# Three token tiles, not two, share the first pass over the up weights

## The chip, the cores and the metric

The kernel runs on one core of a Trainium2 chip. The metric is the device time of one execution in microseconds (us). Engines named below: PE (TensorE, matmuls), DVE (VectorE), ACT (ScalarE), POOL (GpSimd) and SP (SyncE, which issues most transfers).

## The reference

For x of 2048 tokens by 512 features (bf16) the kernel gives x + A(xn) + B(xn), where xn is the layer norm of x over the features without gain or bias:

```
A: Bu = xn @ B_bar^T              complex, 512 states
   h_t = Lam_bar * h_(t-1) + Bu_t over the 2048 tokens
   y   = 2 Re(h @ C^T) + xn * Dskip
B: (silu(xn @ w_gate) * (xn @ w_up)) @ w_down      inner width 1376
```

## The kernel before

Tokens are cut into four chunks of 512, a chunk into four tiles of 128. For chunks 1 to 3 everything is done feature by feature on a transposed chunk. The first tiles of chunk 0 are done token by token, because their work can start before all weights have arrived: a tile of x, transposed on PE against the identity matrix and freed of its mean, is the stationary operand, and a row block of weights, 128 of the 512 input features by 512 columns, is the moving one (`sw_mm`, L503, one matmul for each k, group and tile). The scale of the layer norm (rstd) is applied afterwards, when ACT empties PSUM: `sw_up` (L522) for up, `sw_gate` (L512) for gate. The weight columns stand in three groups: groups 0 and 1 of 512 columns each (`wu01`, `wg01`, loaded row by row, `load_row`, L121), and group 2 of 352 (`w_end`).

In the front, tiles 0 and 1 go together. `raw_mm` (L240) transposes them on PE, `cT_mean` (L244) subtracts the mean by a second matmul into the same PSUM bank, and `raw_copy` (L248), shared by ACT and DVE, brings the centered tile to SBUF. `row_mm` (L747) then does one weight row for both tiles and both groups, four matmuls; the four up rows come first, then the four gate rows. Tile 2 is centered by DVE (`center`, L225), transposed on PE between gate rows 2 and 3, and does its groups 0 and 1 in the list of tile visits (L813), which goes on to group 2 of tiles 0 to 2 and to all of tile 3. The prologue also makes the layer norm's statistics (`ln_stats`, `ln_rstd`), normed tiles (`norm_dve`) and their DMA transposes (`xT0_dma`, L257) for chunk 0, transposes the small parameters on PE (`prm_transpose`, `prm_copy`), and starts the transposed loads of B's two halves (`load_bt`, L148). PE needs B's first half when the visits are done and the projections of chunk 0 (`bproj_tile`, L382) begin.

The order on each engine is the order in which the program is written; there is no scheduler behind it. DVE's and ACT's longer work (tables of sines, statistics and norms of later chunks, the scan `ssm_ops`, the 8 steps `c_ops` that build CF from C) stands in one list, `backlog`. `pump(us)` (L677) is called after every piece of PE work with that piece's length, and takes items from the list as long as the sum of pumped time covers their written costs; `need(tag)` (L691) forces what must be there. An item may have a first part (`pre`), placed up to two items earlier; for CF it is ACT's scaling `cm` (L370), on which DVE's step (L373) waits. A visit of the list at L813 pumps

```
pump(2 * KD * (fgroups[gi][1] - fgroups[gi][0]) * 128 / CW * 0.2163)
```

The norms of a chunk are followed by its DMA transpose (`xT_dma`, L261), for which the projection of that chunk waits. Chunk 3's bias (`ln_nb`, L202), its four norms on ACT (`norm_act`, L212) and its transpose come from the list while PE does the output of chunk 0 (`out_ffn`, `out_ssm`; ACT copies the results, L652); the projection of chunk 3 follows.

Of the kernel before, what the change touches and what calls it, by code (L numbers as in the profile page):

```python
# [11 lines left out]
BF16 = mybir.dt.bfloat16  # L12
ALU = mybir.AluOpType
# [10 lines left out]
def kernel(  # L24
# [17 lines left out]
    nc = tc.nc  # L42
    _, L, D = A_x.shape
# [6 lines left out]
    NCH = L // CW  # L50
    TPC = CW // 128
    KD = D // 128
# [15 lines left out]
    const = ctx.enter_context(tc.tile_pool(name="const", bufs=1))  # L68
# [9 lines left out]
    def bank(shape=(128, CW), dtype=F32):  # L78
        return psum.tile(list(shape), dtype, name="ps")
# [4 lines left out]
    x_v = A_x[0].rearrange("(n p) d -> p n d", p=128)  # L84
# [5 lines left out]
    xall = const.tile([128, NT, D], BF16, name="xall")  # L90
    xnT = const.tile([128, NCH, KD, CW], BF16, name="xnT")
# [29 lines left out]
    def load_row(q, t, view, k):  # L121
        q.dma_start(out=t[:, k, :], in_=view[:, k, 0:FE])  # L122

    HK = KD // 2
    ident = const.tile([128, 128], BF16, name="ident")
    make_identity(nc, ident[:])
    minus_mean = const.tile([128, 128], BF16, name="minus_mean")
# [3 lines left out]
    nc.scalar.preload_act_table_set("silu_and_others")  # L131
    for k in range(KD):
        load_row(nc.sync, wu01, wu_v, k)
    for k in range(HK):
        load_row(nc.sync, wg01, wg_v, k)
    nc.sync.dma_start(out=xall[:, 2, :], in_=x_v[:, 2, :])
    load_row(nc.sync, wg01, wg_v, HK)
    nc.sync.dma_start(out=xall[:, 3, :], in_=x_v[:, 3, :])
    load_row(nc.sync, wg01, wg_v, HK + 1)
# [34 lines left out]
    mv = const.tile([128, NT, 2], F32, name="mv")  # L174
# [10 lines left out]
    def by_k(ap):  # L185
        return ap.rearrange("p (k d) -> p k d", d=128)

    def ln_stats(n):
        nc.vector.bn_stats(out=stats[:, n, 0, :], in_=xall[:, n, :])  # L189
        nc.vector.bn_aggr(out=mv[:, n, :], in_=stats[:, n, 0, :])  # L190
# [6 lines left out]
    def ln_rstd(a, b):  # L197
        nc.vector.tensor_scalar(out=ve[:, a:b], in0=mv[:, a:b, 1], scalar1=EPS, scalar2=None, op0=ALU.add)  # L198
        nc.gpsimd.tensor_tensor(out=rstd[:, a:b], in0=ve[:, a:b], in1=neg_half[:, 0:b - a], op=ALU.pow)  # L199
# [5 lines left out]
    def norm_dve(n):  # L205
        c, i = divmod(n, TPC)
        nc.vector.tensor_scalar(out=xn_tile(c)[:, :, i, :], in0=by_k(xall[:, n, :]), scalar1=mv[:, n, 0:1],
                                scalar2=rstd[:, n:n + 1], op0=ALU.subtract, op1=ALU.mult)
# [9 lines left out]
    SW = TPC - 1  # L218
# [1 line left out]
        return flat(ap).rearrange("p (i k d) -> p k i d", k=KD, i=TPC)  # L220

    xn_c[0], xnT0 = rows_first(xc), rows_first(xnT[:, 0])
    sums = const.tile([128, 2], BF16, name="sums")

    def center(i):  # L225
        nc.vector.tensor_scalar(out=xc[:, i, :], in0=xall[:, i, :], scalar1=mv[:, i, 0:1], scalar2=None, op0=ALU.subtract)

    def sum_dve(i, dst):
        nc.vector.scalar_tensor_tensor(out=xnT[:, NCH - 1, i, 0:HW], in0=xall[:, i, 0:HW], scalar=1.0,
                                       in1=xall[:, i, HW:D], op0=ALU.mult, op1=ALU.add, accum_out=dst)  # L230

    pair = [[[bank() for _ in range(2)] for _ in range(2)] for _ in range(2)]
    warm = pair[0][0][1]
    raw = [pair[0][1] + pair[1][0], pair[1][1] * 2]

    def cT_mm(ps, src, k, first, stop):
        nc.tensor.matmul(ps[:, k * 128:(k + 1) * 128], lhsT=src[:, k * 128:(k + 1) * 128], rhs=ident[:], start=first,  # L237
                         stop=stop)

    def raw_mm(i):  # L240
        for k in range(KD):
            cT_mm(raw[i][k], xall[:, i, :], k, all(p is not raw[i][k] for p in raw[i][:k]), False)

    def cT_mean(i, *ks):  # L244
        nc.tensor.matmul(by_k(raw[i][ks[0]][:])[:, ks[0]:ks[-1] + 1:HK], lhsT=sums[:, i:i + 1].to_broadcast([128, 128]),
                         rhs=minus_mean[:, None, :].to_broadcast([128, len(ks), 128]), start=False, stop=True)

    def raw_copy(i, k):  # L248
        cT_copy(V.tensor_copy if k % 2 else nc.scalar.copy, raw[i][k], i, k, k + 1)

    def cT_copy(copy, ps, i, k0=0, k1=KD):
        copy(out=xcT[:, k0:k1, i * 128:(i + 1) * 128], in_=by_k(ps[:, k0 * 128:k1 * 128]))

    def runs(ap):
        return ap.rearrange("p k (i t) -> p (k i) t", t=128)
# [1 line left out]
    def xT0_dma(i0, i1):  # L257
        nc.sync.dma_start_transpose(out=flat(xnT[:, 0])[:, i0 * D:i1 * D].rearrange("p (n t) -> p n t", t=128),
                                    in_=flat(xc)[:, i0 * D:i1 * D])
# [14 lines left out]
    V = nc.vector  # L274

    def prm_transpose():
        pp = bank()[:, 0:128]
        nc.tensor.matmul(pp, lhsT=prm_rows[:], rhs=ident[:], start=True, stop=True)  # L278
        return pp

    def prm_copy(pp):
        V.tensor_copy(out=prm[:].rearrange("p t q -> p (t q)"), in_=pp[:, 0:3 * NQ])

    def exp_pool(out, in_):
        nc.gpsimd.tensor_tensor(out=out, in0=e_t[:], in1=in_, op=ALU.pow)

    def params_a():
        V.tensor_tensor(out=dre[:], in0=dt_t[:], in1=lre, op=ALU.mult)
        exp_pool(r_t[:], dre[:])
        V.scalar_tensor_tensor(out=ws2[:, 0, :], in0=dt_t[:], scalar=INV_2PI, in1=lim, op0=ALU.mult, op1=ALU.mult)  # L290
# [212 lines left out]
    def sw_mm(ps, groups, gi, i, k0=0, k1=KD):  # L503
        a, b = fgroups[gi]
        for k in range(k0, k1):
            nc.tensor.matmul(ps[:, 0:(b - a) * 128], lhsT=tokens(i, k), rhs=groups[gi][:, k, 0:(b - a) * 128],  # L506
                             start=(k == 0), stop=(k == KD - 1))
# [14 lines left out]
    def sw_up(gi, i, psu):  # L522
        key, h, w = u_home(gi, i)
        if key not in u_pair:
            u_pair[key] = up_p.tile([128, 2, CW], BF16, name="u2")
        nc.scalar.activation(out=u_pair[key][:, h, 0:w], in_=psu[:, 0:w], func=ACT.Copy, scale=sw_scale(i))

    def sw_out(gi, i, psg, psu):
        a, b = fgroups[gi]
        key, h, w = u_home(gi, i)  # L530
        sw_gate(gi, i, psg)
        if psu is not None:
            sw_up(gi, i, psu)
        if h == 1:
            if key[-3:] == "g01":
                g = g0[:, 0:b, i, :].rearrange("p (h f) d -> p h f d", h=2)
                u = u_pair[key][:].rearrange("p h (f d) -> p h f d", d=128)
            else:
                g = g0[:, a:b, i - 1:i + 1, :]
                u = u_pair[key][:, :, 0:w].rearrange("p i (f d) -> p f i d", d=128)  # L540
            products.append(lambda: V.tensor_tensor(out=g, in0=g, in1=u, op=ALU.mult))
# [185 lines left out]
    dummy(warm, 4, CW)  # L727
    dummy(warm, 5, 128)
    nc.vector.tensor_scalar(out=minus_mean[:], in0=ident[:], scalar1=-1.0 / D, scalar2=None, op0=ALU.mult)
    for i in range(2):  # L730
        sum_dve(i, sums[:, i:i + 1])
    raw_mm(0)
    for k in range(HK):
        cT_mean(0, k)
        raw_copy(0, k)
    raw_mm(1)
    for k in range(HK, KD):
        cT_mean(0, k)
    for k in range(HK):
        cT_mean(1, k, k + HK)  # L740
        raw_copy(1, k)
    for k in range(HK, KD):
        raw_copy(0, k)
    for k in range(HK, KD):
        raw_copy(1, k)

    def row_mm(which, k):  # L747
        for i in range(2):
            for gi in range(2):
                sw_mm(pair[which][i][gi], (U, G)[which], gi, i, k, k + 1)  # L750

    for k in range(KD):
        row_mm(0, k)
    for i in range(2):
        ln_stats(i)
        ln_rstd(i, i + 1)
    for gi in range(2):
        for i in range(2):
            sw_up(gi, i, pair[0][i][gi])
    for n in range(2):  # L760
        norm_dve(n)
    row_mm(1, 0)
    pp = prm_transpose()
    ln_stats(2)
    center(2)
    ln_rstd(2, 3)
    ln_stats(3)
    ln_rstd(3, 4)
    prm_copy(pp)
    exp_pool(dt_t[:], ldt)  # L770
    for k in range(1, SW):
        row_mm(1, k)
    t2 = bank()
    for k in range(KD):
        cT_mm(t2, xc[:, 2, :], k, k == 0, k == KD - 1)
    cT_copy(nc.scalar.copy, t2, 2)
    row_mm(1, SW)
    for i in range(2):
        sw_out(0, i, pair[1][i][0], None)
    norm_dve(SW)  # L780
    xT0_dma(SW, TPC)
    norm_dve(2)
    xT0_dma(0, SW)
    params_a()
    load_bt(0)
    load_bt(1)
    nc.gpsimd.iota(out=jidx[:], pattern=[[1, CW]], base=0, channel_multiplier=0,
                   allow_small_or_imprecise_dtypes=True)
    for i in range(2):
        sw_out(1, i, pair[1][i][1], None)  # L790
    tables = table_ops()
    stats1, norm1 = ln_rest(1, False)
    queue("tables", tables[:1])
# [16 lines left out]
        sw_mm(psu, U, gi, i)  # L810
        return psg, psu

    for gi, i in [(0, 2), (1, 2), (2, 0), (2, 1), (2, 2), (0, 3), (1, 3), (2, 3)]:  # L813
        sw_out(gi, i, *sw_both(gi, i))
        if (gi, i) == (2, 0):
            params_sin()
        pump(2 * KD * (fgroups[gi][1] - fgroups[gi][0]) * 128 / CW * 0.2163)
        multiply(1)
# [126 lines left out]
```

## Time and profile before

| | us |
|---|---|
| median of 3 runs | 177.92 (177.83 to 178.49) |
| profiled execution | 178.12 |
| its span, first to last instruction | 176.0 |

The numbers of the trace below come from the profiled execution, counted from the start of its span; its time lies 0.2 above the median and 2.1 above its span. In a row of the timeline stand the start, the length, the engine (PEld: loading of stationary operands; SPq: a transfer issued by SP), the line, the operation, what is written and read, the shape, the number of merged instructions, and in brackets the idle time before and what ended it. A row of the waits has the sum, the count and the longest; a row of the groups has the busy time, the mean in ns, and the idle time before; a row of the transfers ends with the time from issue to landing.

### The profile page before, as it was taken

The numbers are of one execution on the slowest core, as the hardware profiler recorded it, in microseconds if no ns is written. First come the engines' busy times: TensorE is split into PE (matmuls) and PEld (weight loads), VectorE is DVE, ScalarE is ACT, GpSimd is POOL, SyncE is SP. The second block draws the span as 40 slices with busy tenths as digits, with TensorE's granted clock in tenths as the row PEclk, the third lists the DMA queues.
The fourth block names the chain that finished last, engine by engine and source line by source line (L and its number), as shares of the span: only waits on it lengthen the run. The fifth ranks groups of instructions, "written<-read, shape, count | busy, mean of one in ns | idle before, by whom it ended". The sixth has DMA issues, their size and how long they took to land.

```text
span 176.0 us, 2435 instructions
## 1 busy us (share of the span) xinstructions
PE 171.0 (97%) x878; PEld 82.0 (47%) x894; DVE 157.4 (89%) x260; ACT 102.3 (58%) x188; POOL 27.1 (15%) x36
## 2 busy tenths in 40 slices
PE   8899999999999999999999999999999999999993
PEld 5444445564444464444444444446444444444542
DVE  3767999999999999999999999999999999589642
ACT  3179589794996689976044362014666652983100
POOL 5234110022000000000302500014100000530700
PEclk9999999999999999999999999999999999999999
DMA  5998969999999300220005830006310000597741
GB/s 152 370 342 80 194 110 181 303 202 293 169 207 274 115 4 0 50 61 0 2 4 111 94 34 0 0 4 68 53 22 0 0 4 0 70 164 124 93 89 60
DMA packets 34027, 18.05 MB, mean 103 GB/s; under 512 B 24512, under 2 KB 32832, under 8 KB 33888
## 3 DMA queue, kind: packets, MB, share of 16 engines
q1 hardware_dynamic: 30272, 14.39, 35.0%
q0 software_dynamic: 3456, 3.28, 14.6%
q10 hardware_dynamic: 288, 0.23, 0.4%
q8 instruction: 7, 0.11, 0.3%
q14 instruction: 4, 0.03, 0.1%
HBM read 8.33 MB, written 5.24 MB: 77 GB/s over the span
## 4 chain that ended last, share of the span: by engine, by line
PE 94%; DMA 3%; issue 1%; SPq 0%; ACT 0%; DVE 0%; ACTq 0%
PE ps L462 29%; PE ps L630 20%; PE ps L643 16%; PE ps L387 16%; PE ps L506 7%; PE ps L555 3%; DMA wu<-in_B_w_up_dram 3%; PE ps L805 2%; PE ps L620 2%; ACT u L489 0%; SPq L122 0%; SPq L128 0%; DVE xall L646 0%; PE ps L237 0%; PE ps L278 0%
## 5 line engine op out<-in xcount | busy, mean ns | idle before, releaser
L429 DVE TENSOR_TENSOR_SCAN g<-r_t,car,u 128x512 bf16<-128x512 f32 x24 | 28.8, 1263 | 0.0
L643 PE MATMUL ps<-CF,wt 128*128 128x512 bf16 (+2 forms) x133 | 28.2, 366 | 0.2
L387 PE MATMUL ps<-xnT,BT 128*128 128x512 bf16 x125 | 28.1, 379 | 0.2
L630 PE MATMUL ps<-wd_sb,guT 128*128 128x512 bf16 (+2 forms) x129 | 26.5, 362 | 0.1
L462 PE MATMUL ps<-xnT,wu 128*128 128x512 bf16 x94 | 24.5, 379 | 0.2
L462 PE MATMUL ps<-xnT,wg 128*128 128x512 bf16 x93 | 24.3, 379 | 0.1
L389 ACT CAST u<-ps 128x512 bf16<-128x512 f32 x32 | 17.8, 591 | 5.0 <-PE ps L387 4.1
L489 ACT CAST u<-ps 128x512 bf16<-128x512 f32 x30 | 17.8, 592 | 4.8 <-PE ps L462 4.8
L643 PEld LDWEIGHTS <-wt 128*128 128x128 bf16 x136 | 12.9, 98 | 15.0 <-DVE xall L600 0.4
L387 PEld LDWEIGHTS <-BT 128*128 128x128 bf16 x128 | 12.5, 98 | 14.9 <-DMA BT<-in_A_B_re_dram 0.3
L630 PEld LDWEIGHTS <-guT 128*128 128x128 bf16 x130 | 12.4, 98 | 13.8
L199 POOL TENSOR_TENSOR rstd<-ve,neg_half 128x1 f32<-128x1 f32 (+1 forms) x7 | 7.0, 1001 | 73.0 <-DVE ve L198 72.6
L652 ACT CAST res<-ps 128x512 bf16<-128x512 f32 x12 | 6.9, 582 | 18.5 <-PE ps L643 18.5
L592 ACT ACTIVATE xr<-xall,nb,rstd 128x512 bf16<-128x512 bf16 x16 | 11.8, 804 | 8.7 <-DVE xall L600 5.0
L653 POOL DMA_DIRECT2D out_dram<-res x12 | 10.5, 1043 | 35.6 <-ACT res L652 30.0
L462 PEld LDWEIGHTS <-wu 128*128 128x128 bf16 x96 | 9.4, 98 | 11.3
L488 ACT ACTIVATE guT<-ps 128x512 bf16<-128x512 f32 x20 | 12.1, 604 | 4.0 <-PE ps L462 3.6
L462 PEld LDWEIGHTS <-wg 128*128 128x128 bf16 x96 | 9.3, 98 | 10.6
L212 ACT ACTIVATE xn<-xall,nb,rstd 128x512 bf16<-128x512 bf16 x8 | 6.3, 816 | 8.8 <-DVE nb L202 8.8
L189 DVE BATCH_NORM_STATS2 stats<-xall 128x6 f32<-128x512 bf16 x16 | 10.8, 675 | 0.6 <-DMA xall<-in_A_x_dram 0.6
L462 PE MATMUL ps<-xnT,w_end 128*128 128x512 bf16 x47 | 10.8, 379 | 0.1
L397 DVE TENSOR_TENSOR pm<-g,c 128x2048 bf16<-128x2048 bf16 x8 | 9.8, 1222 | 0.1
(132 smaller groups left out, 235.3 us busy)
## 6 DMA issues: line engine op xcount, KB each, us to landing
out_dram<-in_A_x_dram SPq DMA_DIRECT2D x8, 192.0 KB, 3.2
out_dram<-res POOLq DMA_DIRECT2D x12, 128.0 KB, 3.1
out_dram<-xall POOLq DMA_DIRECT2D x3, 512.0 KB, 6.4
wd_sb<-in_B_w_down_dram SPq DMA_DIRECT2D x1, 1280.0 KB, 7.8
wu<-in_B_w_up_dram SPq DMA_DIRECT2D x4, 256.0 KB, 4.9
wg<-in_B_w_gate_dram SPq DMA_DIRECT2D x4, 256.0 KB, 5.5
xall<-in_A_x_dram SPq DMA_DIRECT2D x1, 1024.0 KB, 7.0
xall<-in_A_x_dram SPq DMA_DIRECT2D x1, 512.0 KB, 6.1
```

The costliest lines, as they stand in the source:

```text
L189: nc.vector.bn_stats(out=stats[:, n, 0, :], in_=xall[:, n, :])
L387: nc.tensor.matmul(ps[:] if c else by_k(ps[:]), lhsT=BT[:, part, k, q * 128:(q + 1) * 128], rhs=xnT[:, c, k, :] if c else xnT0[:, k], star ...
L389: nc.scalar.copy(out=u_tiles[c][:, part, q, :], in_=ps[:])
L429: V.tensor_tensor_scan(out=g()[:, part, q, :], data0=r_t[:, q:q + 1].to_broadcast([128, CW]), data1=u_tiles[c][:, part, q, :], initial=ini ...
L462: nc.tensor.matmul(ps[:fs, lo:hi], lhsT=wslice(groups, fi, k), rhs=xnT[:, c, k, lo:hi], start=(k == 0), stop=(k == KD - 1))
L488: nc.scalar.activation(out=gu(c, fi, fi + 1)[:fs, 0, :], in_=psg[:fs], func=ACT.Silu)
L489: nc.scalar.copy(out=u_pair[c][:fs, fi % 2, :], in_=psu[:fs])
L506: nc.tensor.matmul(ps[:, 0:(b - a) * 128], lhsT=tokens(i, k), rhs=groups[gi][:, k, 0:(b - a) * 128], start=(k == 0), stop=(k == KD - 1))
L592: nc.scalar.activation(out=box["xr"][:], in_=xall[:, n, :], func=ACT.Identity, scale=rstd[:, n:n + 1], bias=nb[:, n:n + 1])
L630: nc.tensor.matmul(o_tiles[n, b][:, 0:hi - lo], lhsT=gu(c, fi, fi + 1)[:, 0, i * 128:(i + 1) * 128], rhs=wd_sb[:, fi, lo:hi], start=(fi == ...
L643: nc.tensor.matmul(o[:, 0:hi - lo], lhsT=w_tiles[c][:, part, q, i * 128:(i + 1) * 128], rhs=CF[:, part, q, lo:hi], start=False, stop=(part ...
L653: nc.gpsimd.dma_start(out=out_v[:, n, lo:hi], in_=res[:, lo:hi], accum_op=ALU.add)
```

## The change

- Tile 2 of x is loaded on SP's queue between up rows 0 and 1, before it came after gate row 1.
- Tiles 0, 1 and 2 share the passes over up and gate. Six PSUM banks hold up, and gate tiles reuse banks. For row 0, tiles 0 and 1 go first; tile 2's transposes, copies, mean and row 0 follow; rows 1 to 3 go over three tiles.
- The mean is no longer added in PSUM by matmuls into the transposed tile. `raw_copy` now copies the raw transposed tile on ACT alone, in two halves; one matmul for each tile (`mean_mm`) makes the negative mean, and DVE adds it (`centered`). `center` and tile 2's later transposes are gone.
- Gate runs tile by tile instead of row by row, each tile over all four rows.
- The parameters' transpose stands behind up row 2, their copy behind tile 0's statistics; all statistics of chunk 0 come before its norms.
- The visits (0, 2) and (1, 2) leave the list of tile visits, and with them their calls of `pump`.

```diff
+        if k == 0:
+            nc.sync.dma_start(out=xall[:, 2, :], in_=x_v[:, 2, :])
     for k in range(HK):
         load_row(nc.sync, wg01, wg_v, k)
-    nc.sync.dma_start(out=xall[:, 2, :], in_=x_v[:, 2, :])
...
+    upb0 = [bank() for _ in range(2)]
+    raw = [bank() for _ in range(SW)]
+    low01, low2 = bank(), bank()
+    upb = [upb0, raw[0:2], [raw[2], bank()]]
+    gateb = [[low01, low2], upb[0], upb[1]]
+    xrT = xnT[:, NCH - 2]
...
+    def raw_copy(i, h):
+        k0, k1 = h * HK, (h + 1) * HK
+        nc.scalar.copy(out=xrT[:, k0:k1, i * 128:(i + 1) * 128], in_=by_k(raw[i][:, k0 * 128:k1 * 128]))
+    def mean_mm(i):
+        nc.tensor.matmul(mean_of(i), lhsT=sums[:, i:i + 1].to_broadcast([128, 128]), rhs=minus_mean[:], start=i != 1,
+                         stop=i != 0)
+    def centered(i, k0, k1):
+        at = slice(i * 128, (i + 1) * 128)
+        V.tensor_tensor(out=xcT[:, k0:k1, at], in0=xrT[:, k0:k1, at],
+                        in1=mean_of(i)[:, None, :].to_broadcast([128, k1 - k0, 128]), op=ALU.add)
...
+    for i in range(2):
+        raw_mm(i)
+        mean_mm(i)
+        for h in range(2):
+            raw_copy(i, h)
     for k in range(HK):
+        for i in range(2):
+            centered(i, k, k + 1)
+    for i in range(2):
+        for gi in range(2):
+            up_mm(i, gi, 0)
+    raw_mm(2)
+    for h in range(2):
+        raw_copy(2, h)
+    sum_dve(2, sums[:, 2:3])
+    mean_mm(2)
     for k in range(HK):
+        centered(2, k, k + 1)
+    for gi in range(2):
+        up_mm(2, gi, 0)
+    for i in range(SW):
+        centered(i, HK, KD)
+    for k in range(1, KD):
+        for i in range(SW):
             for gi in range(2):
+                up_mm(i, gi, k)
+        if k == HK:
+            pp = prm_transpose()
+    for i in range(SW):
         ln_stats(i)
         ln_rstd(i, i + 1)
+        if i == 0:
+            prm_copy(pp)
+            exp_pool(dt_t[:], ldt)
+    for i in range(SW):
+        for k in range(KD):
+            for gi in range(2):
+                sw_mm(gateb[i][gi], G, gi, i, k, k + 1)
+        if i < 2:
+            for gi in range(2):
+                sw_up(gi, i, upb[i][gi])
     ln_stats(3)
     ln_rstd(3, 4)
+    for n in (0, 1, SW, 2):
+        norm_dve(n)
+        if n == SW:
+            xT0_dma(SW, TPC)
     xT0_dma(0, SW)
+    for gi in range(2):
+        sw_out(gi, 0, gateb[0][gi], None)
+    for gi in range(2):
+        sw_up(gi, SW - 1, upb[SW - 1][gi])
+    for gi in range(2):
+        sw_out(gi, 1, gateb[1][gi], None)
...
-    for gi, i in [(0, 2), (1, 2), (2, 0), (2, 1), (2, 2), (0, 3), (1, 3), (2, 3)]:
+    for gi, i in [(2, 0), (2, 1), (2, 2), (0, 3), (1, 3), (2, 3)]:
```

More of the change, by code (lines that the diff above doesn't have):

```diff
@@ L222 @@
     xn_c[0], xnT0 = rows_first(xc), rows_first(xnT[:, 0])
-    sums = const.tile([128, 2], BF16, name="sums")
-    def center(i):
-        nc.vector.tensor_scalar(out=xc[:, i, :], in0=xall[:, i, :], scalar1=mv[:, i, 0:1], scalar2=None, op0=ALU.subtract)
+    sums = const.tile([128, SW], BF16, name="sums")
     def sum_dve(i, dst):
@@ L230, in sum_dve @@
                                        in1=xall[:, i, HW:D], op0=ALU.mult, op1=ALU.add, accum_out=dst)
-    pair = [[[bank() for _ in range(2)] for _ in range(2)] for _ in range(2)]
-    warm = pair[0][0][1]
-    raw = [pair[0][1] + pair[1][0], pair[1][1] * 2]
+    upb0 = [bank() for _ in range(2)]
[3 more added lines that the diff above has]
+    gateb = [[low01, low2], upb[0], upb[1]]
+    warm = upb0[0]
+    xrT = xnT[:, NCH - 2]
     def cT_mm(ps, src, k, first, stop):
@@ L241, in raw_mm, with mean_of @@
         for k in range(KD):
[L242 to L252, printed above, removed]
+            cT_mm(raw[i], xall[:, i, :], k, k == 0, k == KD - 1)
+    def raw_copy(i, h):
+        k0, k1 = h * HK, (h + 1) * HK
+        nc.scalar.copy(out=xrT[:, k0:k1, i * 128:(i + 1) * 128], in_=by_k(raw[i][:, k0 * 128:k1 * 128]))
+    def mean_of(i):
+        return low2[:, 0:128] if i == SW - 1 else low01[:, i * 128:(i + 1) * 128]
+    def mean_mm(i):
[5 more added lines that the diff above has]
+                        in1=mean_of(i)[:, None, :].to_broadcast([128, k1 - k0, 128]), op=ALU.add)
     def runs(ap):
@@ L276, in prm_transpose @@
     def prm_transpose():
-        pp = bank()[:, 0:128]
+        pp = low2[:, 128:256]
         nc.tensor.matmul(pp, lhsT=prm_rows[:], rhs=ident[:], start=True, stop=True)
@@ L729, with up_mm @@
     nc.vector.tensor_scalar(out=minus_mean[:], in0=ident[:], scalar1=-1.0 / D, scalar2=None, op0=ALU.mult)
+    def up_mm(i, gi, k):
+        sw_mm(upb[i][gi], U, gi, i, k, k + 1)
     for i in range(2):
         sum_dve(i, sums[:, i:i + 1])
-    raw_mm(0)
-    for k in range(HK):
[L734 to L738, printed above, removed]
-    for k in range(HK):
[L740 to L748, printed above, removed]
+    for i in range(2):
[3 more added lines that the diff above has]
+            raw_copy(i, h)
+    for k in range(HK):
+        for i in range(2):
[8 more added lines that the diff above has]
+    mean_mm(2)
@@ L749, in row_mm @@
+    for k in range(HK):
+        centered(2, k, k + 1)
[5 more added lines that the diff above has]
+        for i in range(SW):
             for gi in range(2):
[L750 to L754, printed above, removed]
+                up_mm(i, gi, k)
+        if k == HK:
+            pp = prm_transpose()
+    for i in range(SW):
@@ L755 @@
         ln_stats(i)
         ln_rstd(i, i + 1)
[L757 to L766, printed above, removed]
+        if i == 0:
[8 more added lines that the diff above has]
+                sw_up(gi, i, upb[i][gi])
@@ L767 @@
     ln_stats(3)
     ln_rstd(3, 4)
[L769 to L782, printed above, removed]
-    xT0_dma(0, SW)
+    for n in (0, 1, SW, 2):
+        norm_dve(n)
+        if n == SW:
+            xT0_dma(SW, TPC)
@@ L788 @@
                    allow_small_or_imprecise_dtypes=True)
-    for i in range(2):
-        sw_out(1, i, pair[1][i][1], None)
+    for gi in range(2):
+        sw_out(gi, SW - 1, gateb[SW - 1][gi], None)
     tables = table_ops()
```

## Prediction

> **What bounds the kernel now.** First the page (busy shares, and the chain of work that ended last), then PE's waits, then the timeline of the first 25 us, then the stretch around chunk 3's projection, because that is where the vector engine's (DVE's) work meets PE's again.
>
> ```profile
> PE 171.0 (97%) x878; PEld 82.0 (47%) x894; DVE 157.4 (89%) x260; ACT 102.3 (58%) x188; POOL 27.1 (15%) x36
> PE 94%; DMA 3%; issue 1%; SPq 0%; ACT 0%; DVE 0%; ACTq 0%
> PE ps L506 <- DMA wu<-in_B_w_up_dram: 0.6, 1, 0.6
> ```
>
> PE is the bound: 94% of the chain is PE, and its one real wait is 0.6 us for up row 1. So every new PE stall is paid in full, and the change can win little more than that wait. DVE, at 89%, is close behind.
>
> The front, in time order (start, length, then engine and line):
>
> ```profile
> 0.78 2.40 PE L703 MATMUL ps<-const-bfloat16-1.0 128*128 128x512 bf16 x9 [0.78 <-PEq L929]
> 3.09 0.61 PE L237 MATMUL ps<-ident,xall 128*128 128x128 bf16 x4
> 3.48 0.43 DVE L229 SCALAR_TENSOR_TENSOR xnT<-xall 128x256 bf16<-128x256 bf16 x1
> 4.82 1.07 PE L506 MATMUL ps<-wu,CF 128*128 128x512 bf16 x4
> 4.85 0.60 ACT L252 CAST CF<-ps 128x128 bf16<-128x128 f32 x3 [0.69 <-PE ps L245]
> 5.06 0.69 DVE L252 CAST CF<-ps 128x128 bf16<-128x128 f32 x3 [0.78 <-PE ps L245]
> 5.67 0.68 DVE L189 BATCH_NORM_STATS2 stats<-xall 128x6 f32<-128x512 bf16 x1
> 6.49 2.75 PE L506 MATMUL ps<-wu,CF 128*128 128x512 bf16 x12 [0.60 <-DMA wu<-in_B_w_up_dram]
> 6.67 0.68 DVE L189 BATCH_NORM_STATS2 stats<-xall 128x6 f32<-128x512 bf16 x1
> 12.15 0.58 ACT L252 CAST CF<-ps 128x512 bf16<-128x512 f32 x1 [1.03 <-PE ps L237]
> 16.27 2.75 PE L805 MATMUL ps<-w_end,CF 128*128 128x512 bf16 x12
> ```
>
> A 512-column matmul costs 0.216 us (twelve from 6.49 to 9.08), a 128-column one 0.055.
>
> **Part 1, tile 2 in the first row.** The new chain to the first up matmul is transpose, ACT copy, DVE addition of the mean. Tile 1's sum ends at about 3.9, so its mean matmul ends near 4.4; ACT's two-block copies cost about 0.37 each (between the 128-column and the 512-column cast), the last needed one ending near 4.7; the DVE additions, not in this trace, I take at the cast's price, 0.28 (0.2 apart in a row). So tile 0 starts near 4.8 as now, and tiles 0 and 1 end near 5.7. Then tile 2: five small matmuls (0.28), drain 0.2, copy 0.37, addition 0.28, three handovers: row 0 of tile 2 starts near 6.9 and row 1 near 7.3. Left from there are 42 matmuls of 0.216 and one small one, 9.1: the first w_end matmul comes at 16.4 instead of 16.27. **+0.15.** The old 0.6 wait is gone, and tile 2's own 0.9 stands in its place.
>
> This needs tile 2's x by 5.7. Its new place on SP is right behind row 0:
>
> ```profile
> wu<-in_B_w_up_dram SPq DMA_DIRECT2D x1, 256.0 KB, 2.9
> wu<-in_B_w_up_dram SPq DMA_DIRECT2D x1, 256.0 KB, 4.8
> ```
>
> Row 0 (issued 1.2) took 2.9 to land, row 1 (issued 1.65) 4.8. Tile 2 issued at 1.65 lands between 4.6 (the first's latency) and 6.5 (the second's). I take under 5.7; the late end costs 0.55 more. Rows 1 to 3 and gate rows 0 and 1 land some 0.37 later (half a row's spacing), row 1 at about 6.8, before PE asks; the second gate row has two us in hand. The transfers behind keep their order.
>
> **Part 2, B's transpose.** The parameter copy now stands on DVE between tile 0's and tile 1's statistics, behind PE's third up row.
>
> ```profile
> 12.51 1.02 POOL L285 TENSOR_TENSOR dt_t<-e_t,prm 128x4 f32<-128x4 f32 x1
> 12.58 0.73 DVE L207 TENSOR_SCALAR CF<-xall,mv,rstd 128x512 bf16<-128x512 bf16 x2 [0.58 <-POOL rstd L199]
> 13.02 2.70 SPq L258 DMA_TRANSPOSE xnT<-CF  x2
> 15.77 4.41 SPq L150 DMA_TRANSPOSE BT<-in_A_B_re_dram  x1
> BT<-in_A_B_re_dram SPq DMA_TRANSPOSE x1, 7.3
> 22.31 1.03 PE L805 MATMUL ps<-w_end,xnT 128*128 128x512 bf16 x4
> 23.10 6.65 PEld L387 LDWEIGHTS <-BT 128*128 128x128 bf16 x32 [0.26 <-DMA BT<-in_A_B_re_dram]
> ```
>
> Row 2 of three tiles ends at 7.3 + 12 x 0.216 = 9.9; the copy runs at 10.15. Then three blocks of statistics at 1.0 each (5.67 to 6.67), the wait for tile 3's power (0.58) and its norm (0.40): 14.4, where the transpose now issues at 13.02. Tile 3's transpose therefore issues 1.4 later, and behind it on SP stand the other transpose and B's first half: 17.1 instead of 15.77, landing at 24.4 if the 7.3 holds. PE wants it at 23.17 + 0.15. Now it lands just in time (0.26 of idle weight loading, no PE gap), so **+1.05**. Bounds: 0 (the 7.3 holds queueing behind older transfers, which by then are gone) to 1.4.
>
> If B is early, chunk 1's transpose asks for nearly the same toll: three more products stand ahead of its norms on DVE. I count one of the two.
>
> **Part 3, the planner.** The two leading entries of the list of tile visits, (0,2) and (1,2), are gone, and each called the pump with 2 x 4 x 512/512 x 0.2163 = 1.73. So 3.46 us of queued work is handed out later for good: in the built order each later DVE and ACT step stands about two feature tiles further on. Where DVE was late anyway this costs nothing; where ACT interleaves it with evacuations, it does.
>
> ```profile
> 8.70 2.42 ACT L526 ACTIVATE u<-ps,rstd 128x512 bf16<-128x512 f32 x4 [3.25 <-PE ps L506]
> 13.93 0.69 DVE L541 TENSOR_TENSOR guT<-guT,u 128x1024 bf16<-128x1024 bf16 x1
> 15.37 0.88 DVE L301 TENSOR_SCALAR pm<-jidx,ws 128x512 f32<-128x512 f32 x2 [0.75 <-POOL jidx L787]
> 16.17 0.69 DVE L189 BATCH_NORM_STATS2 stats<-xall 128x6 f32<-128x512 bf16 x1
> 23.17 7.07 PE L387 MATMUL ps<-xnT,BT 128*128 128x512 bf16 x32
> 67.31 4.06 DVE L373 SCALAR_TENSOR_TENSOR CF<-CT,nc2im,cm 128x512 bf16<-128x512 bf16 x6
> 71.76 1.42 DVE L373 SCALAR_TENSOR_TENSOR CF<-CT,nc2im,cm 128x512 bf16<-128x512 bf16 x2
> L370 ACT ACTIVATE cm<-CT,nc2re 128x512 f32<-128x512 bf16 x4 | 3.0, 743 | 0.0
> L488 ACT ACTIVATE xnT<-ps 128x512 bf16<-128x512 f32 x4 | 2.4, 603 | 0.0
> L560 ACT ACTIVATE g_last<-ps 128x192 bf16<-128x192 f32 x2 | 0.7, 336 | 0.0
> 90.11 0.14 DVE L202 SCALAR_TENSOR_TENSOR nb<-mv,rstd 128x4 f32<-128x4 f32 x1
> 90.28 2.93 ACT L212 ACTIVATE xn<-xall,nb,rstd 128x512 bf16<-128x512 bf16 x4 [7.12 <-DVE nb L202]
> L652 ACT CAST res<-ps 128x512 bf16<-128x512 f32 x12 | 6.9, 582 | 18.5 <-PE ps L643 18.5
> 93.24 1.97 SPq L262 DMA_TRANSPOSE xnT<-xn  x1
> xnT<-xn SPq DMA_TRANSPOSE x1, 4.3
> 99.44 1.89 PE L387 MATMUL ps<-xnT,BT 128*128 128x512 bf16 x8
> ```
>
> Up to chunk 3's bias (nb, L202) the built order holds the same DVE work as before apart from the front, so its new time is 90.1 plus what DVE loses:
> - Front: tile 1's power stands on POOL behind the 1.02 one for dt, so ACT has tile 1's rstd near 12.0; from there ACT has two scalings of tile 1, two gates of tile 0 and two scalings of tile 2 to do (0.58 apart, 2.42 for four) before tile 1's first gate (0.7). The first product starts near 16.3, and by then DVE has done neither it nor the two turns that it had done by 16.17: 0.1 + 0.65 + 0.88 = **1.65**.
> - The first sine stands behind seven of chunk 0's eight evacuations instead of three (0.86 apart, 7.07 for eight), and the next table step reuses its buffer. Between 0 and 3.4; I take **1.2**, as DVE is itself 2 us later.
> - The eight CF steps wait for ACT's eight scalings cm. Those stood up to three in a row; now they stand one or two between the pairs of evacuations (0.60 each, overlapping: about 0.95 a pair). Three more pairs fall inside the run, less the two short pairs of the remainder tile (0.34 each, about 0.4 a pair): **2.1**, between 0 and 2.9.
>
> Sum 5.0: nb at 95.1. Behind it ACT's four norms, 2.93, now alternate with two of the out tiles' copies (0.58 each, 0.5 apart): done at 99.2, transpose issued there, 4.3 to land: 103.5. PE reaches chunk 3's projection at 99.44 + 0.15 + 1.05 = 100.6, where it had 1.9 us in hand (93.24 + 4.3 = 97.55). **+2.9 to 3.0.** If the last two terms are nothing, nb comes at 91.8 and the transposed tile at 100.2: no stall. If both are at their upper ends, 2.9 + 3.0 = 5.9.
>
> Sum: 0.15 + 1.05 + 3.0 = 4.2. The profiled execution took 178.12 (span 176.0), so 182.3; the median of the runs, 177.92, gives **182.1**. A stall behind 103 I do not expect: PE is then 4.2 late, DVE 5.0, and DVE waits for PE at the end.
>
> **Rivals.**
> - *The late stall is small or absent* (ACT and DVE make up the second and third terms): 0.15 + 1.05 to 2.7, 179.1 to 180.6. For it: ACT is 58% busy. Against it: ACT has no gap between 64 and 75 us. 0.17.
> - *The clock.* The nine warm-up matmuls took 2.40 us, half pace; the matmuls at 4.82 run at full pace. Now PE idles some 0.6 us just before that point. If full pace comes one stretch as long as the warm-up later (about 3.4 from 4.9), ten long matmuls and five short ones lose 0.21 and 0.05 each, less what tile 2's wait hides: +1.2 to 2.0, 183.3 to 184.1 in all. 0.08. The Trainium skill, "TensorE: Matmul & The Clock Gate", Part 1, has the clock released only after a busy window of about 3.4 us that runs freely; by that rule the idle 0.6 can spoil the window, and the time would be this rival's. The trace agrees with half pace at the start and cannot show how much idle a window bears.
> - *Faster.* Tile 2's preparation hides fully behind tiles 0 and 1 and B's transpose queues less: the 0.6 wait goes, and five small matmuls fewer save 0.27: 177.0. It decides if tile 2's addition is ready by 6.0 and nb by 92. Against it: the chain of part 1 is serial and 1.2 long. 0.03.
> - *Nothing measurable*: B in time and no late stall, 178.1. 0.05.
>
> **How the numbers follow.** The forecast, 181.2 to 183.2, has 0.67, the rivals the rest. About 0.5% (0.9 us) is what a measurement here can tell from no change. Below 180.0 lies about 0.16 and above 183.8 about 0.04, so the range is 180.0 to 183.8. Slower by over 0.5%: 0.67 + 0.17 + 0.08 = 0.92; within 0.5%: 0.05; faster: 0.03.
>
> **What would show it.** PE's waits: a gap of 0.7 to 1.1 before tile 2's first up matmul, about 1 before the first projection (or before chunk 1's), about 3 before chunk 3's, released through chunk 3's transpose. nb of chunk 3 near 95 and the CF steps waiting on ACT. PE gaplessly reaching chunk 3's projection with nb near 92 would prove the third part wrong; 128-column matmuls at half pace after 5 us would make it the clock.

## The result: 187.55 us, 5.4% slower, and the profile after

Six runs of the changed kernel have a median of 187.55 us (186.60 to 190.62), six of the kernel before beside them 177.88 (177.66 to 178.49): ratio 1.0537, 95% interval 1.0474 to 1.0600 (ratios here and below leave out runs over 1.5% above the fastest of their kernel, here 190.62). The prediction said 182.1, between 180.0 and 183.8. The direction was right, the size less than half of what came.

The profiled execution took 190.62 us (span 188.6), the longest of the six. Its page: TensorE's (PE's) and DVE's busy shares, the granted clock in 40 slices, the chain that ended last by engine; and PE's waits (total, times, longest):

```profile
PE 178.1 (94%) x891; PEld 82.9 (44%) x891; DVE 159.0 (84%) x266; ACT 103.2 (55%) x189; POOL 27.4 (15%) x36
PEclk9999999999999999999999958999999999999999
PE 87%; DMA 8%; DVE 2%; ACT 1%; issue 0%; SPq 0%
PE ps L395 <- DMA xnT<-xn: 5.5, 2, 4.8
PE ps L514 <- DVE CF L259: 0.7, 1, 0.7
```

Three things are new. DMA holds 8% of the chain, 6 of them the transposes xnT<-xn, for which PE waits 0.7 us before chunk 1's projection and 4.8 before chunk 3's. The clock falls in the 24th and 25th slice, 108 to 118 us. And the span is 12.6 us longer, more than PE's waits make (about 7). The timeline has the rest, first at the front, then around chunk 3:

```profile
4.96 1.86 PE L514 MATMUL ps<-wu,CF 128*128 128x512 bf16 x4 [0.48 <-DMA wu<-in_B_w_up_dram]
8.04 5.37 PE L514 MATMUL ps<-wu,CF 128*128 128x512 bf16 x14 [0.68 <-DVE CF L259]
19.77 2.54 PE L818 MATMUL ps<-w_end,CF 128*128 128x512 bf16 x11
98.54 0.14 DVE L203 SCALAR_TENSOR_TENSOR nb<-mv,rstd 128x4 f32<-128x4 f32 x1
103.08 2.87 SPq L270 DMA_TRANSPOSE xnT<-xn  x1
109.28 9.83 PE L395 MATMUL ps<-xnT,BT 128*128 128x512 bf16 x32 [4.80 <-DMA xnT<-xn]
```

At the front 512-column matmuls run at half pace until about 12.4 (the fourteen from 8.04 take 5.2 us up to the next, where 14 x 0.216 = 3.0 would do; the 2.2 lost are ten matmuls at half pace), and the first w_end matmul comes at 19.77 instead of 16.27. The row of the granted clock shows nothing of that: its first slices read 9, in both kernels, though the warm-up runs at half pace too. There the matmuls' own durations have to be read. Chunk 3's tile, asked for at 103.08, lets PE start only at 109.28. The 32 matmuls behind the stall then take 9.83 us; the same 32 take 7.08 where the clock is up (the third experiment, below).

So three suspects: the clock at the front, the stall, and the clock behind the stall. One profile can't say which of them every execution pays.

### The profile page after: what moved, and what is told of

Same layout as the page of the kernel before. It is cut to its first block, busy times and chain, and to the rows that moved or that the text cites. A ratio compares the mean times of both kernels' runs of the same rounds, so it can differ in the third digit from the quotient of the medians.

```text
span 188.6 us, 2454 instructions
## 1 busy us (share of the span) xinstructions
PE 178.1 (94%) x891; PEld 82.9 (44%) x891; DVE 159.0 (84%) x266; ACT 103.2 (55%) x189; POOL 27.4 (15%) x36
## 4 chain that ended last, share of the span: by engine, by line
PE 87%; DMA 8%; DVE 2%; ACT 1%; issue 0%; SPq 0%
PE ps L470 27%; PE ps L638 18%; PE ps L651 14%; PE ps L395 13%; PE ps L514 9%; DMA xnT<-xn 6%; PE ps L563 2%; DMA wu<-in_B_w_up_dram 2%; PE ps L818 2%; PE ps L628 1%; DVE xn L208 1%; DVE pm L318 1%; DVE pm L317 0%; PE ps L239 0%; DVE guT L549 0%
## 5 line engine op out<-in xcount | busy, mean ns | idle before, releaser
L395 PE MATMUL ps<-xnT,BT 128*128 128x512 bf16 x128 | 31.1, 405 | 5.8 <-DMA xnT<-xn 5.5
L395 PEld LDWEIGHTS <-BT 128*128 128x128 bf16 x128 | 13.0, 104 | 23.4 <-DMA xnT<-xn 6.2
L405 DVE TENSOR_TENSOR pm<-u,c 128x2048 bf16<-128x2048 bf16 x8 | 9.8, 1222 | 0.1
```

Source lines behind the costliest of these rows:

```text
L395: nc.tensor.matmul(ps[:] if c else by_k(ps[:]), lhsT=BT[:, part, k, q * 128:(q + 1) * 128], rhs=xnT[:, c, k, :] if c else xnT0[:, k], star ...
```

## The experiments

| kernel | us, median (range) | against the kernel before |
|---|---|---|
| changed | 187.55 (186.60 to 190.62) | 1.0537 (1.0474 to 1.0600) |
| 1: changed, front filled | 187.49 (186.83 to 188.09) | 1.0544 (1.0508 to 1.0580) |
| 2: changed, pump back | 179.00 (178.58 to 182.45) | 1.0067 (1.0046 to 1.0087) |
| 3: changed, stall filled | 185.04 (183.87 to 187.28) | 1.0385 (1.0342 to 1.0428) |
| 4: 1 and 2 together | 178.77 (178.45 to 179.55) | 1.0058 (1.0030 to 1.0086) |
| 5: 1, without chunk 0's stores | 184.63 (184.28 to 184.85) | 1.0379 (1.0362 to 1.0397) |
| 6: before, less the two pumps | 186.26 (185.77 to 186.82) | 1.0468 (1.0442 to 1.0494) |
| 7: before, shorter warm-up | 178.12 (177.23 to 178.73) | 1.0008 (0.9990 to 1.0025) |
| 8: 2, rows reordered, B early | 178.50 (177.80 to 180.47) | 1.0031 (1.0012 to 1.0050) |
| 9: 8 with more pump | 180.39 (179.46 to 180.94) | 1.0152 (1.0122 to 1.0181) |
| 10: changed, once more | 187.01 (186.02 to 188.04) | 1.0519 (1.0469 to 1.0568) |

**1. The front's gaps filled.**

```diff
+    dummy(warm, 5, 128)            # ahead of the first up matmul
...
     mean_mm(2)
+    dummy(upb[2][1], 10, 128)      # ahead of tile 2's first
```

> The changed kernel with five 128-column dummy matmuls ahead of the first up matmul and ten ahead of tile 2's first, so that the TensorE hardly idles between 0.8 and 8 us; nothing else differs. Clock theory (the two idle stretches of 0.48 and 0.68 us hold the clock at half pace until about 12.9): 512-column matmuls at 0.216 from about 5 us on, first w_end matmul at 16.3 to 16.8 instead of 19.77, 3.0 to 3.5 us less: 184.0 to 184.6. Rival (row 0's landing and tile 2's chain set the front, the clock is late for another reason): half pace until 12 us as before, first w_end matmul at 19.7 to 20.3, 187.5 to 188.2.

The profile did what the clock theory said: full pace from about 5, the first w_end matmul at 16.43.

```profile
6.87 3.19 PE L514 MATMUL ps<-wu,CF 128*128 128x512 bf16 x14
16.43 2.75 PE L820 MATMUL ps<-w_end,CF 128*128 128x512 bf16 x12
```

The time did not follow: 187.49, no change of the median, where the theory said 184.0 to 184.6 and the rival, whose mechanism the profile refutes, 187.5 to 188.2. Only the spread shrank, from 4.0 us to 1.3. The changed kernel once more, the tenth run, gives the reason.

> The changed kernel as it is, once more, to see how often the front stays at half pace. If the two idle stretches at the front decide by chance (whether a stretch of the clock gate falls on them), executions fall into a group at 186 to 187.5 with the first w_end matmul near 16.4, and one at 189 to 191 with it near 19.8; the half pace behind the stall is in every one. If the front's half pace is in all of them, none is under 188.

Its profiled execution (187.59 us) has the same two gaps in PE's timeline, and the clock comes up all the same:

```profile
4.76 1.44 PE L514 MATMUL ps<-wu,CF 128*128 128x512 bf16 x4 [0.45 <-DVE CF L259]
7.21 3.19 PE L514 MATMUL ps<-wu,CF 128*128 128x512 bf16 x14 [0.73 <-DVE CF L259]
16.77 2.75 PE L818 MATMUL ps<-w_end,CF 128*128 128x512 bf16 x12
33.26 7.08 PE L395 MATMUL ps<-xnT,BT 128*128 128x512 bf16 x32 [0.88 <-DMA xnT<-xn]
95.54 0.14 DVE L203 SCALAR_TENSOR_TENSOR nb<-mv,rstd 128x4 f32<-128x4 f32 x1
100.08 3.01 SPq L270 DMA_TRANSPOSE xnT<-xn  x1
106.61 9.44 PE L395 MATMUL ps<-xnT,BT 128*128 128x512 bf16 x32 [5.14 <-DMA xnT<-xn]
```

Fourteen up matmuls in 3.19 us, the first w_end matmul at 16.77. So the half pace at the front is a matter of chance: the first profile drew it, and of the ten runs only that one and one of 189.32, of which there is no trace, lie over the 188.20 of the next. The second experiment's profile drew it as well (w_end at 20.14, 182.45 us where its seven other runs have 178.58 to 179.41); the third's, with the same unfilled front, did not (16.31). None of the four runs came out at 189 to 191, so the two groups that were expected are not seen here; the half pace behind the stall is in all four, whose mean clock is 0.982 or 0.991. That the two gaps cause the chance is likely and not shown: the thirteen runs with a filled front (experiments 1, 4 and 5) have no such outlier, but at two in ten that happens by luck about once in 18 times. From here on this tenth profile is the one to read. Its stall and slow projection are much like the first's.

**2 and 4. The planner's time given back, alone and with the filled front.**

```diff
+    pump(4 * KD * 0.2163)
     for gi, i in [(2, 0), (2, 1), (2, 2), (0, 3), (1, 3), (2, 3)]:
```

> The changed kernel with the 3.46 us that the two removed visits gave the planner handed out again, in one call ahead of the tile visits. Planner theory: chunk 3's bias comes some 3.4 us earlier against the TensorE, the stall before chunk 3's projection falls from 4.8 to between 0 and 1.5, and with it the half pace of the projection behind it (2.9): 180.0 to 182.7. Rival (the vector engine is late because the front was late, by the clock): the stall stays over 3, 185.5 to 187.5.

> Both of the first two edits. If clock at the front and planner are separate causes, the savings add: 3.0 to 3.5 and 4.8 to 7.0, 177.1 to 179.8. If the late vector engine has one cause only, the sum is that of the larger alone, 180 to 182.

One line takes 8.5 us away, to 179.00, below even the 180.0 to 182.7 that were expected. Neither profile has a wait over 0.4 us before any projection, chunk 1's among them. The fourth is at the same place, 178.77. That lies within the range for savings that add, but they don't: the first saved nothing at the median, and the second alone made nearly all of it. From the fourth's timeline:

```profile
68.97 4.06 DVE L381 SCALAR_TENSOR_TENSOR CF<-CT,nc2im,cm 128x512 bf16<-128x512 bf16 x6
91.76 0.14 DVE L203 SCALAR_TENSOR_TENSOR nb<-mv,rstd 128x4 f32<-128x4 f32 x1
94.88 1.88 SPq L270 DMA_TRANSPOSE xnT<-xn  x1
95.82 0.95 POOL L661 DMA_DIRECT2D out_dram<-res  x1 [7.24 <-ACT res L660]
100.47 7.08 PE L395 MATMUL ps<-xnT,BT 128*128 128x512 bf16 x32 [0.40 <-DMA xnT<-xn]
```

The six CF steps run without a gap again, and nb stands at 91.76: 1.65 behind the kernel before. The pumped time is here what it was there, so this is the new front's own share.

**6. The planner's part on the old kernel.**

```diff
-        pump(2 * KD * (fgroups[gi][1] - fgroups[gi][0]) * 128 / CW * 0.2163)
+        if (gi, i) not in ((0, 2), (1, 2)):
+            pump(2 * KD * (fgroups[gi][1] - fgroups[gi][0]) * 128 / CW * 0.2163)
```

> The kernel before without the pump calls of the visits (0,2) and (1,2), everything else as it was. Planner theory (3.46 us of queued work handed out later is the cause by itself): chunk 3's bias comes at 92.8 to 94.3 instead of 90.11, its norms alternate with the out copies, its transpose is issued at 97 to 98.7 and lands 4.3 to 6.4 later: a stall of 1.8 to 5.5 before chunk 3's projection, above about 3.4 the half pace behind it too: 180 to 186, most likely 184. Rival (it takes the late front as well): under 179.

186.26, just over the range: with the old front and the old visits, two calls less make 8.4 of the 9.7 us. The order of DVE's and ACT's work is all that they set. Its timeline:

```profile
32.03 7.08 PE L387 MATMUL ps<-xnT,BT 128*128 128x512 bf16 x31 [0.95 <-DMA xnT<-xn]
68.98 0.75 DVE L373 SCALAR_TENSOR_TENSOR CF<-CT,nc2im,cm 128x512 bf16<-128x512 bf16 x1 [0.67 <-ACT cm L370]
77.24 0.75 DVE L373 SCALAR_TENSOR_TENSOR CF<-CT,nc2im,cm 128x512 bf16<-128x512 bf16 x1 [0.78 <-ACT cm L370]
94.32 0.14 DVE L202 SCALAR_TENSOR_TENSOR nb<-mv,rstd 128x4 f32<-128x4 f32 x1
98.85 2.71 SPq L262 DMA_TRANSPOSE xnT<-xn  x1
104.90 10.01 PE L387 MATMUL ps<-xnT,BT 128*128 128x512 bf16 x31 [4.66 <-DMA xnT<-xn]
```

The CF steps start 1.67 later than before (67.31) and end 4.8 later (77.99 against 73.18): they wait for ACT's scalings. nb is 4.21 later. All the rest follows: the stall of 4.66, the long projection, and chunk 1's wait of 0.95 too.

**3. The stall filled with matmuls.**

```diff
     out_chunk(0)
+    dummy(bank(), 16, CW)
     bproj_chunk(3)
```

> The changed kernel with sixteen 512-column dummy matmuls between chunk 0's out tiles and chunk 3's projection (3.5 us at full pace). Clock theory (4.8 us of idle TensorE brings the half pace of the first 13 projection matmuls): they run at 0.216, the projection takes 6.9 to 7.1 instead of 9.83, the transposed tile lands no later: 184.7 to 186.2. Rival (the projection is slow for another reason, its evacuations or its weights): it still takes 9 to 10 us, 187.5 or more.

185.04, 2.5 less than the changed kernel. The transposed tile lands no earlier, but PE idles 1.83 and not 5, and the projection runs at full pace:

```profile
106.33 7.08 PE L395 MATMUL ps<-xnT,BT 128*128 128x512 bf16 x32 [1.83 <-DMA xnT<-xn]
```

So the idle itself, not the projection's work, brings the half pace, and that costs 2.4 to 2.75 in these two profiles (9.44 and 9.83 less 7.08).

**5. Without the stores beside the transpose.**

```diff
+                if c:
                     nc.gpsimd.dma_start(out=out_v[:, n, lo:hi], in_=res[:, lo:hi], accum_op=ALU.add)
```

> The changed kernel with the filled front of the first experiment, and without the four stores of chunk 0's out tiles (its output lacks them); nothing else differs. Contention theory (the stores issued at 96.5 to 101.6 lengthen chunk 3's transpose, issued at 99.28, from 4.3 to 6.4; and an idle TensorE of 5 us, but not one of 3, brings the half pace): the transpose lands 4.2 to 4.5 behind its issue, the stall is 2.8 to 3.1, the projection runs at full pace: 2.1 and 2.65 less than the first experiment, 182.3 to 183.2. If 3 us of idle TensorE bring the half pace too: 184.8 to 185.7. Rival (the transpose is long for another reason, its own issue among them): 187 to 188.

184.63: the mechanism is that of the second case, 0.2 under its range, with the transpose short and the half pace there all the same. First the DMA view (median us from issue to landing) of this run and, behind it, that of the tenth; each is for the stretch 88 to 108 us:

```profile
xnT<-xn SPq DMA_TRANSPOSE x1, 4.3
```

```profile
out_dram<-res POOLq DMA_DIRECT2D x4, 128.0 KB, 3.7
xnT<-xn SPq DMA_TRANSPOSE x1, 6.5
```

Without company the transpose takes 4.3 us again, and the stall is 2.94, the size that was predicted. With the four stores around it, two of them issued before it, it takes 6.5. Where the first store is issued 0.94 behind it (the fourth experiment, 95.82 against 94.88), it takes 5.5; where 1.36 behind (the second, below), 4.3. From the second's timeline, and its DMA view for the same stretch:

```profile
98.30 1.87 SPq L270 DMA_TRANSPOSE xnT<-xn  x1
99.66 0.95 POOL L661 DMA_DIRECT2D out_dram<-res  x1 [7.67 <-ACT res L660]
```

```profile
xnT<-xn SPq DMA_TRANSPOSE x1, 4.3
```

By the Trainium skill, "DMA: Bandwidth & Descriptors", section "Queues, rings and completion order", each DMA engine takes turns between its queues, a packet at a time. This comparison agrees in so far as the stores cost the transpose time, 6.5 against 4.3; it doesn't show the packets.

But the half pace didn't go. PE's busy time and granted clock, by stretches (start and end, length, busy, clock, DMA share, GB/s), first here, then in the changed kernel's first profile:

```profile
98.00:101.30 3.30, 3.30 (x16) 1.00 0.04 8
101.30:103.48 2.18, 0.02 (x1) 1.00 1.15 213
103.48:104.26 0.78, 0.00 (x1) 0.50 0.22 45
104.26:106.89 2.63, 2.63 (x7) 0.50 0.00 0
106.89:110.00 3.11, 3.11 (x16) 1.00 0.00 0
```

```profile
104.47:108.05 3.58, 0.00 (x1) 1.00 1.09 172
108.05:109.28 1.23, 0.00 (x1) 0.50 1.08 150
109.28:114.88 5.60, 5.60 (x14) 0.50 0.01 1
114.88:118.00 3.12, 3.12 (x16) 1.00 0.00 0
```

The half pace lasts 3.41 us here and 6.83 there: one and two of the same unit. In the first the clock falls 2.18 us after PE's last matmul, 0.78 before work returns, and costs half of 2.63. In the second PE works 2.2 us of the first unit, which isn't enough, and waits for a second. The Trainium skill, "TensorE: Matmul & The Clock Gate", Part 1, has a window of about 3.4 us that runs freely, and the clock lowered after an idle window. The unit agrees. But a window of that length that ended at 103.48 held 1.2 us of work (3.41 less 2.18) and still counted as idle: what a window bears is less than the page's sentence suggests. The runs' mean clocks tell the two lengths apart. In the tenth experiment 186.02 and 186.43 have a clock of 0.991 (0.009 x 2 x 184 = 3.3 us of half pace), 187.59 and 188.04 have 0.982 (6.7); between the pairs lie 1.6 us, about half of the unit. That the second unit costs so much is not shown by it: among the sixth experiment's runs 186.10 has 0.990 and the shorter 185.77 has 0.981.

**7. Is the old front near the edge?**

```diff
-    dummy(warm, 5, 128)
```

> The kernel before without its five 128-column warm-up matmuls, which leaves the TensorE idle for some 0.5 us ahead of the raw transposes at 3.1. If so little idle can spoil a stretch of the clock gate, some executions keep half pace until 8 to 9 us and are 1.5 to 2.5 longer, 179.4 to 180.4, others are as before: the runs spread over two values. If it cannot: 177.6 to 178.3 in every run.

A miss on both sides: the median doesn't move, and ten runs spread over 1.5 us with no two groups, but six of them lie outside 177.6 to 178.3. The profile does show half pace until about 7.4 (sixteen up matmuls where the kernel before has four, the wait for row 1, and twelve), and the first w_end matmul at 16.78 instead of 16.27:

```profile
4.86 4.90 PE L506 MATMUL ps<-wu,CF 128*128 128x512 bf16 x16
```

The half pace costs 1.3 us there (4.73 to the next matmul, 16 x 0.216 = 3.46), and up row 1, for which PE waits anyway, hides 0.8 of it.

**8 and 9. Is there a version that beats both?**

```diff
-    for i in range(2):
-        for gi in range(2):
-            up_mm(i, gi, 0)
+    for k in range(HK):            # x of tile 2 now behind up row 1
+        for i in range(2):
+            for gi in range(2):
+                up_mm(i, gi, k)
     raw_mm(2)
...
+    for i in range(2):
+        for gi in range(2):
+            up_mm(i, gi, HK)       # ahead of tile 2's rows 0 to 2
...
+    load_bt(0)                     # ahead of tile 3's transpose
+    pump(4 * KD * 0.2163)          # the ninth: 6 in place of 4, and
+                                   # dummy(warm, 4, 128) ahead of row 0
```

> The changed kernel with the planner's 3.46 us given back, x of tile 2 behind up row 1, rows 0 to 2 of tiles 0 and 1 ahead of tile 2's first matmul (so that tile 2's chain lies beside them), and B's first half asked for ahead of tile 3's transpose. If tile 2's wait is what this front still costs: first w_end matmul at 15.7 to 16.0 where the kernel before has 16.27; if then B's half lands in time, 177.4 to 178.2. If the vector engine's later norms set chunk 1's or chunk 3's transposes: 178.3 to 179.3.

> The eighth experiment's kernel (rows reordered, B's first half early, planner's time given back) with one feature tile's 1.73 us more handed to the planner ahead of the visits, and four 128-column dummy matmuls ahead of the first up matmul. If the 0.67 stall before chunk 3's projection (transpose issued at 94.27, in company with the stores) is what is left, the bias comes some 1.5 us earlier, the stall goes and the front's spread with it: 177.3 to 177.9, at or just under the kernel before. If the earlier work on the vector engine only takes another place in its queue (the products of the visits come later, and the TensorE waits for them): 178.3 or more.

The eighth, in which tile 3's norm also goes ahead of the others, does what was meant at the front: tile 2's chain costs PE nothing, and the first w_end matmul comes at 15.93, 0.34 ahead of the kernel before:

```profile
15.93 2.75 PE L822 MATMUL ps<-w_end,CF 128*128 128x512 bf16 x12
```

It ends at 178.50 all the same, 0.3% over. Its chunk 3 transpose, issued at 94.27 with a store 0.75 behind, takes 5.6 and stalls PE for 0.67. The ninth, with more pumped, is worse by 1.9. PE's wait, and ACT's timeline at that place:

```profile
PE ps L395 <- ACT u L534: 1.4, 1, 1.4
29.38 1.06 ACT L322 ACTIVATE c<-pm 128x1024 bf16<-128x1024 f32 x1 [1.86 <-DVE pm L318]
30.34 0.37 ACT L522 ACTIVATE guT<-ps 128x256 bf16<-128x256 f32 x1
30.61 0.38 ACT L534 ACTIVATE u<-ps 128x256 bf16<-128x256 f32 x1
```

A sine pulled forward waits for DVE 1.86 us at the head of ACT's queue, the evacuations behind it come late, and chunk 0's projection waits 1.43 for a bank. The stall before chunk 3's, which was to go, stays at 0.68. The first w_end matmul comes 0.55 later than in the eighth's profile (16.48); whether the added dummies have a part in that, no run tells. Pumping is not good or bad in itself; it has to match where the other engines are. No version here beat the kernel before.

## Why the prediction was wrong

Its steps against the tenth profile, whose time is 9.47 over the kernel before's profiled 178.12:

| step | predicted | measured |
|---|---|---|
| front, to the first w_end matmul | +0.15 | +0.50 (16.77); 0.04 in the third experiment |
| from there to the end of chunk 0's out tiles (B, chunk 1) | +1.05 | +1.53 (101.47 against 99.44, less 0.50) |
| nb of chunk 3 | 95.1 | 95.54 |
| its transpose issued | 99.2 | 100.08 |
| issue to landing | 4.3 | 6.48 |
| stall before chunk 3's projection | 3.0 | 5.14 |
| the projection behind the stall | 0 | +2.36 (9.44 less 7.08) |
| sum | 4.2 | 9.53 |

*Part 1* was right in mechanism and, where the clock is up, nearly in size. Tile 2's own wait is 0.73 where 0.9 was said. The clock rival, given 0.08, exists, but by chance: two or so executions in ten, and at 3.0 to 3.5 (19.77 against 16.77 and 16.31 with the same front), not 1.2 to 2.0: full pace came at about 12.4, where the rival had 8.3 (4.9 + 3.4).

*Part 2* had nearly the right toll, mostly in another place. B's half, issued at 17.63, landed 6.3 later and not 7.3, and PE's weight loading waited 0.6 for it: chunk 0's projection came 7.21 behind the first w_end matmul and not 6.90, which is 0.31. Most of the rest stood before chunk 1's projection, 0.88 of idle time, as the alternative said. But its cause is the planner and not the parameter copy or the products: the sixth experiment has it (0.95) with the old front, the fourth has the new front and none. In the first experiment's profile PE instead waits 0.69 before chunk 0's projection, for ACT's evacuations, and not before chunk 1's.

*Part 3* named the mechanism, the place and the chain. Its terms were these: 1.65 for the front, which the fourth experiment shows (that it fits to the hundredth is luck: this profile's front is 0.46 late and not 0.15); 1.2 and 2.1 for the sine order and the CF steps, where the sixth shows 1.67 up to the CF steps, the sine's part not taken apart, and 3.1 in them, partly made up before nb (4.21 together). The sum for nb was 0.4 off.

**The step that failed** is what came behind nb: "transpose issued there, 4.3 to land: 103.5", and the 3.0 taken as the whole price of the stall. The 4.3 is from a row in which the transpose ran ahead of the stores; the prediction itself moved it among them, by letting the norms alternate with the out copies, and didn't reprice it: 2.18. And it knew the clock rule well enough to price the front by it, but didn't put the same question to the stall that it forecast itself: 2.36. Those two and 0.8 ahead of the stall are the missing 5.3. The fifth experiment shows the first by itself (4.3, stall 2.94), the third the second by itself. The fifth also shows that a stall of the size that was forecast, 2.94, can bring a half pace by itself: 1.3 us, and all four of its runs have the lower clock.

Left open: what decides whether the front's clock is late, and how much work a stretch of the clock gate must hold. Here a stretch with 1.2 us of work before the fall counted as idle, and 1.83 us of idle time in all did no harm; at half pace 2.2 us of work in one didn't raise the clock, and 2.6 did. More than these bounds the runs don't give.

## What to carry to other kernels

A loop's entry can be worth more for what it hands out than for its matmuls: when work leaves a loop that feeds a planner, move its time too, and compare the order of every engine's work to the end of the kernel. A stall has two prices: its length, with its transfer's duration taken among its new neighbours, and the half pace of what follows when PE idles some 3 us. One profiled execution is one draw: where a chance is in play, see a second before blaming what the first shows.

## What was not expected of the hardware

A 16-block DMA transpose takes 4.3 us by itself, and 5.5 to 6.7 when 128 KB accumulating stores of another queue are issued ahead of it or up to 0.94 us behind it; with the first store 1.36 behind it or later, 4.3 again. The half pace came 2.18 us after PE's last matmul in the fifth experiment and 3.1 to 3.8 after it in the four other profiles that have it (the changed kernel's two, the first and the sixth experiment); it lasted 3.41 us in the fifth and 6.83 in those four, nothing between. At the front the same order of matmuls is at full pace from about 5 to 5.6 us in the third and tenth profiles (gaps of 0.45 and 0.73 us) and from 12.4 and 13 in the changed kernel's first and the second experiment's (0.45 to 0.48 and 0.68).
